# Scaling of the coarse attention probabilities moved from VectorE to GpSimd, with three schedule constants

## The chip, the cores and the metric

One core of a Trainium2 chip runs the whole program: two attentions, their sum and two feed-forward layers. The metric is the device time of one execution in microseconds (us).

## The reference, cut to what matters

Shapes: q, k and v are 2 x 8 x 576 x 64 (batch, heads, positions, head size); the feed-forward layers have 1152 tokens, width 512 and inner width 2048.

```python
q_d = q.reshape(B, H, Sd, factor, D).mean(axis=3)      # factor 4, so Sd = 144; k_d and v_d alike
out_d = sm_attn(q_d, k_d, v_d)                         # softmax attention over 144 coarse positions
out_up = np.repeat(out_d, factor, axis=2)
mask = np.abs(pos[:, None] - pos[None, :]) < factor    # fine attention in a band of 7 positions
...
attn = np.exp(scores)
attn = attn / (np.sum(attn, axis=-1, keepdims=True) + 1e-09)
out_local = np.matmul(attn, v)
x = out_up + out_local                                 # then token by token, heads side by side
h = x @ w_in;  g = P(h) / (Q(h) + 1e-06);  x = g @ w_out      # first layer, rational function
h = x @ w_in2; g = h * np.tanh(softplus(h)); out = g @ w_out2 # second layer
```

The division in the coarse softmax is what the change moves: the kernel multiplies the exponentials by the reciprocal of their sum.

## The kernel before, in words

The kernel is built as a list of tasks with estimated durations, priorities and dependencies (`Plan.add`). A list scheduler (`Plan.run`, L105) then walks through an estimated time and gives each free engine the ready task with the lowest priority number; in that order the instructions are written out. So every engine has a fixed instruction order, chosen once, and on the chip each engine runs its list strictly in order, waiting on semaphores.

Attention is cut into 24 units (`unit`, L550): two heads by 2, 3 or 4 windows of 64 positions. Units 1 to 4 have 4 windows and belong to the first quarter of the tokens, units 5 to 12 to the second (3 and 2 windows in turn), 13 to 16 to the third, 17 to 24 to the fourth. Per unit: TensorE transposes q (L467); VectorE sums q over groups (L595) and GpSimd scales the sums (L610); TensorE forms fine and coarse scores (L630 to L641); VectorE takes maxima (L651, L652); ScalarE takes exponentials with their sums (L658, L662); VectorE takes reciprocals of the five sums (L670, L673). Then two scalings follow: `ns` (L678) of the fine probabilities, 128 x 80 per window, on GpSimd or VectorE as the scheduler finds it; and `npd` (L684) of the coarse ones, 128 x 144, on VectorE. Both precede TensorE's transposes of the probabilities (L696 of the coarse, L700 of the fine), which are copied out of PSUM (L712, L717), multiplied with v (L731 coarse, L737 fine) and added up (L749, L756) into x, which is split in two float32 parts xh (L767/L769) and xl (L772).

`prep` (L469) serves each pair of heads in each batch: k is loaded (L475/L479) and transposed, v is loaded (L530, "vr") and its four-fold sums are formed in two additions (L536, L540) on GpSimd or VectorE. Every load is issued from SyncE's queue (SP): q by L564, the v windows of a unit by L576, the weights by L866 and L871. q has three buffers (`NQN = 3`), so from the fourth q load on a load waits until an earlier unit's q has been transposed.

The feed-forward layers run in steps of two blocks of 128 inner columns: L1003 is the first matmul of a step (three products for float32 accuracy), L1151 and L1153 the second. Weights arrive in a wide format and are decoded by ScalarE and VectorE: L883, L890, L897 (and L903), then split into a high part (L909 on ScalarE or L911 on VectorE) and a low part (L914). The first L1003 of a step needs that step's decoded weights, its x, and a free PSUM buffer. Where TensorE has no task the scheduler may place a filler matmul (L448, 128 x 480 bfloat16, result unused).

What sets the order around the change: the priority of units (`PROL`, `PSTEP` for the first four, `LEAD` for all others, L833 and L835: how far ahead of its feed-forward step a unit is wanted), of the v windows (`VOFF`, L581), of weight decoding (`CLEAD`, L918), and the estimated durations (`t_pool`, `t_dve`, `t_act`).

Of the kernel before, what the change touches and what calls it, by code (L numbers as in the profile page):

```python
# [25 lines left out]
SECOND = 0.8  # L26
COLD, FILL_ALL = 3.4, 20
WINDOW, FILL, FILL_END = 3.4, 0.5, 450.0
LEAD, CLEAD, LLEAD, OLAG = 25, 5, 35, 16
PROL, PSTEP, VOFF, VROFF, LOFF, KOFF = -45, 1.5, 0, 0, 11, 12  # L30
GROUPS = ([6, 6, 4], [4, 4, 4, 4])
KCUT = 4
MKP = -45
# [10 lines left out]
def t_dve(n, fast=False, ptr=0):  # L44
    return 0.068 + n * (0.000521 if fast else 0.001042) + 0.06 * ptr


def t_pool(n, two=True):
    return 0.147 + n * 0.0021 if two else 0.06 + n * 0.00104
# [22 lines left out]
class Plan:  # L72
# [6 lines left out]
    def add(self, engs, fn, prio, after=(), take=(), use=(), chain=None, dens=0.5, port=False):  # L79
        t = Task()  # L80
        t.port = port
        t.dens = dens
        t.engs, t.fn, t.prio, t.take = engs, fn, prio, list(take)
        t.out, t.next, t.started, t.ended, t.seq = [], None, False, False, len(self.tasks)
        t.use = list(take) + list(use)
        deps = set(after)
        for b in take:
            b.owner = t
        for b in use:
            deps.add(b.owner)  # L90
        for b in t.use:
            b.users += 1
        deps.discard(None)
        t.deps = len(deps)
        if chain is not None:
            if chain in self.last:
                self.last[chain].next = t
                t.deps += 1
            self.last[chain] = t
        for d in deps:  # L100
            d.out.append(t)
        self.tasks.append(t)
        return t
# [134 lines left out]
def kernel(  # L238
# [13 lines left out]
    nc = tc.nc  # L252
# [6 lines left out]
    SD = S // 4  # L259
# [4 lines left out]
    add = plan.add  # L264
# [285 lines left out]
    def unit(u, slots, start):  # L550
        bb, p, w0, nw, n, prio = u.bb, u.p, u.w0, u.nw, u.n, u.prio
# [5 lines left out]
        tm, s, pd, pT, pdT, od, xt = (  # L557
            Buf(tm_s), Buf(s_s), Buf(pd_s), Buf(pT_s), Buf(pdT_s), Buf(od_s), Buf(xt_s)
        )
# [66 lines left out]
        def pe_b():  # L626
# [19 lines left out]
            use=[qT, qd], chain="pb",  # L646
# [28 lines left out]
        tc_ = add({"dve": 0.35}, rc, prio, after=[te], use=[tm])  # L675
# [5 lines left out]
            )  # L681

        def npd():
            nc.vector.tensor_scalar(  # L684
                out=pd.v, in0=pd.v, scalar1=tm.v[:, 14:15], scalar2=0.25, op0=ALU.mult,
                op1=ALU.mult,
            )

        tn = [
            add({"pool": t_pool(WK * nw), "dve": t_dve(WK * nw)}, ns, prio, after=[tc_], use=[tm, s], port=True),  # L690
            add({"dve": 0.2}, npd, prio, after=[tc_], use=[tm, pd], port=True),
        ]

        def pe_d():
# [31 lines left out]
        def pe_e():  # L726
# [17 lines left out]
            use=[vw, pT, pdT], chain="pe",  # L744
# [85 lines left out]
    for c in range(4):  # L830
        for i, (bb, p, w0, nw) in enumerate(need[c]):
            if c == 0:
                prio = PROL + PSTEP * i  # L833
            else:
                prio = cstart[c - 1] + (i / len(need[c])) * (cstart[c] - cstart[c - 1]) - LEAD  # L835
            slots = {"half": half_s, "s": sc_s, "pt": pt_s, "po": po_s}
            if c == 0:
                slots = {kk: slots[kk] + early[kk] for kk in slots}
            if (bb, p) not in seen:
                seen.add((bb, p))  # L840
                prep(bb, p, prio - 1, slots, c == 0)
            att_last = unit(Unit(bb, p, w0, nw, prio), slots, c == 0)
# [435 lines left out]
```

## Time and profile before

| | us |
|---|---|
| time, median of 3 runs (lowest to highest) | 513.7 (509.99 to 514.14) |
| the profiled execution | 511.9 |
| its span, first to last instruction | 510.1 |
| TensorE busy | 494.1 (97%) |
| VectorE, ScalarE busy | 351.7 (69%), 346.0 (68%) |
| GpSimd busy | 77.6 (15%) |

The span is the profiled execution without some 1.8 us around it. "Busy" of TensorE is modelled, since matmuls are pipelined. The shares are averages over an attention-heavy first quarter and a second half that is nearly matmuls alone, so they are read by stage below.

### The profile page before, as it was taken

The page shows a single profiled execution, that of the slowest core. Times are in us where ns is not written, and L with a number is a line of the kernel's source. Part 1 is how long each engine was busy: PE and PEld are TensorE (multiplying, and loading weights), DVE is VectorE, ACT ScalarE, POOL GpSimd, SP SyncE. Part 2 cuts the span into 40 slices and gives each one's busy share as a digit, 9 for nine tenths or more (in the row PEclk, how much of TensorE's full clock was granted, in tenths as well). Part 3 has the DMA queues.
Part 4 walks back from the last instruction along what each step waited for, and adds up shares of the span by engine and source line. Part 5 has one row for each costly group of instructions (what it writes and reads, how often), then busy time and mean ns, then how long its engine had stood idle before and what let it go on. Part 6 is the DMA issues. An engine that isn't in the chain of part 4 may idle for free.

```text
span 510.1 us, 8850 instructions
## 1 busy us (share of the span) xinstructions
PE 494.1 (97%) x3503; PEld 447.8 (88%) x3503; DVE 351.7 (69%) x530; ACT 346.0 (68%) x648; POOL 77.6 (15%) x104
## 2 busy tenths in 40 slices
PE   8989999999999999999989999999999999999996
PEld 5668668889999999999979989888998899989995
DVE  4778999899899996898889998925832622221322
ACT  5789997998889999999998999655621422112210
POOL 3644556334000000000000403400000000000000
PEclk9989999999999999999989999999999999999999
DMA  9986835241322242222412224252300000000111
GB/s 179 200 235 179 199 100 183 56 112 45 143 84 84 82 164 84 84 82 84 126 41 84 82 92 156 84 164 84 131 36 0 1 0 1 0 1 0 63 62 62
DMA packets 44313, 46.51 MB, mean 91 GB/s; under 512 B 27760, under 2 KB 30832, under 8 KB 44272
## 3 DMA queue, kind: packets, MB, share of 16 engines
q1 hardware_dynamic: 44272, 45.95, 30.4%
q8 instruction: 27, 0.44, 0.3%
q14 instruction: 14, 0.11, 0.1%
HBM read 43.58 MB, written 2.36 MB: 90 GB/s over the span
## 4 chain that ended last, share of the span: by engine, by line
PE 55%; ACT 23%; DVE 15%; issue 3%; DMA 3%; POOL 0%; SPq 0%; DVEq 0%; POOLq 0%; ACTq 0%
PE psum L1003 22%; PE psum L1153 19%; PE psum L1151 6%; ACT L945 2%; ACT raw L890 2%; ACT wt L883 2%; ACT wrk L1029 2%; DMA att<-in_v_dram 2%; DVE wt L897 1%; ACT att L658 1%; DVE wi L914 1%; DVE wrk L1039 1%; PE psum L467 1%; DMA raw<-in_moe_w_in_dram 1%; PE psum L448 1%
## 5 line engine op out<-in xcount | busy, mean ns | idle before, releaser
L1003 PE MATMUL psum<-xh,wi 128*128 128x384 f32 (+1 forms) x528 | 132.9, 324 | 0.0
L1003 PEld LDWEIGHTS psum<-xh,wi 128*128 128x128 f32 x528 | 93.7, 188 | 1.8 <-issue 1.2
L1003 PE MATMUL psum<-xl,wi 128*128 128x384 f32 (+1 forms) x264 | 84.5, 320 | 0.0
L1003 PE MATMUL psum<-xh,late_r 128*128 128x384 f32 x288 | 77.0, 336 | 2.1 <-DVE late_f L1047 1.2
L1151 PE MATMUL psum<-gg,wo 128*128 128x384 f32 (+1 forms) x456 | 73.7, 316 | 2.7 <-ACT gg L1118 1.7
L1151 PEld LDWEIGHTS psum<-gg,wo 128*128 128x128 f32 x456 | 69.8, 192 | 4.4 <-DVE gg L1123 2.1
L1003 PEld LDWEIGHTS psum<-xh,late_r 128*128 128x128 f32 x288 | 52.4, 188 | 3.5 <-DVE late_f L1047 1.5
L1153 PE MATMUL psum<-wo,gg 128*128 128x512 f32 x216 | 51.0, 391 | 0.0
L1003 PEld LDWEIGHTS psum<-xl,wi 128*128 128x128 f32 x264 | 49.8, 189 | 0.2
L1003 PE MATMUL psum<-xl,late_r 128*128 128x384 f32 x144 | 48.2, 335 | 0.0
L1153 PEld LDWEIGHTS psum<-wo,gg 128*128 128x128 f32 x216 | 40.4, 188 | 8.1
L1097 ACT ACTIVATE late_f<-psum 128x768 f32<-128x768 f32 (+1 forms) x12 | 9.5, 790 | 53.1 <-PE psum L1003 53.1
L897 DVE SCALAR_TENSOR_TENSOR wt<-wt,raw 128x1024 int32<-128x1024 int32 x32 | 40.5, 1269 | 7.0 <-ACT raw L890 3.8
L890 ACT ACTIVATE raw<-raw 128x1024 int32<-128x1024 uint16 x32 | 36.8, 1154 | 9.1 <-DMA raw<-in_moe_w_in_dram 5.8
L1210 POOL TENSOR_TENSOR xl<-part,xh 128x768 fp32r<-128x768 f32 x6 | 15.6, 2616 | 177.2 <-ACT xh L1205 177.2
L883 ACT ACTIVATE wt<-raw 128x1024 f32<-128x1024 f32 x32 | 36.4, 1140 | 7.8 <-DMA raw<-in_moe_w_out_dram 4.0
L1230 DVE TENSOR_TENSOR part<-psum,part 128x512 f32<-128x512 f32 x27 | 18.3, 692 | 32.7 <-PE psum L1153 32.7
L1097 ACT ACTIVATE wrk<-psum 128x768 f32<-128x768 f32 (+1 forms) x13 | 10.3, 790 | 44.6 <-PE psum L1003 44.6
L1123 DVE TENSOR_TENSOR gg<-wrk,gg 128x768 fp32r<-128x768 f32 (+2 forms) x23 | 19.5, 852 | 19.9 <-ACT gg L1097 19.6
L1003 PEld LDWEIGHTS psum<-xl,late_r 128*128 128x128 f32 x144 | 27.0, 188 | 0.3
L1153 PE MATMUL psum<-wo,late_r 128*128 128x512 f32 x108 | 25.6, 390 | 0.0
L1123 DVE TENSOR_TENSOR gg<-late_f,gg 128x768 fp32r<-128x768 f32 x14 | 13.4, 955 | 17.6 <-ACT gg L1097 17.2
(133 smaller groups left out, 980.0 us busy)
## 6 DMA issues: line engine op xcount, KB each, us to landing
raw<-in_moe_w_in_dram SPq DMA_DIRECT2D x16, 1024.0 KB, 5.1
raw<-in_moe_w_out_dram SPq DMA_DIRECT2D x16, 1024.0 KB, 4.9
out_dram<-part SPq DMA_DIRECT2D x9, 256.0 KB, 2.1
att<-in_v_dram SPq DMA_DIRECT2D x32, 60.0 KB, 2.5
att<-in_k_dram SPq DMA_DIRECT2D x6, 288.0 KB, 4.6
att<-in_v_dram SPq DMA_DIRECT2D x6, 256.0 KB, 5.2
att<-in_q_dram SPq DMA_DIRECT2D x16, 96.0 KB, 4.1
att<-in_v_dram SPq DMA_DIRECT2D x8, 80.0 KB, 5.6
```

Source lines behind the costliest of these rows:

```text
L883: nc.scalar.activation(out=t.v, in_=words(r)[:, :, 1].bitcast(F32), func=AF.Prelu if fold else AF.Identity, scale=2.0 ** -112, **({"alpha" ...
L890: nc.scalar.activation(out=words(r)[:, :, 0], in_=r.v.bitcast(U16).rearrange("p (n four) -> p n four", four=4)[:, :, 1], func=AF.Copy, sca ...
L897: nc.vector.scalar_tensor_tensor(out=ti, in0=ti, scalar=3, in1=words(r)[:, :, 0], op0=ALU.logical_shift_left, op1=ALU.bitwise_or)
L945: nc.scalar.preload_act_table_set(name)
L1003: nc.tensor.matmul(st.h.v[:, i, :T], w.v[:, ww, ks], xx[:, kk, c0:c0 + T], start=(nn == 0 and (st.big or i == 0)), stop=(nn == 3 * KD - 1 ...
L1029: nc.scalar.activation(out=vw(st.a), in_=H(), func=AF.Abs)
L1097: nc.scalar.activation(out=vw(dst), in_=H(), func=AF.Mish)
L1123: ENG[e].tensor_tensor(out=vw(st.gl), in0=vw(st.c), in1=vw(st.gh).bitcast(F32), op=ALU.subtract)
L1151: nc.tensor.matmul(A(d)[:, :T], w.v[:, ww, lo + d * 128:lo + (d + 1) * 128], vw(gg)[:, i, :], start=start, stop=stop)
L1153: nc.tensor.matmul(A(d), vw(gg)[:, i, sl], w.v[:, ww, lo:lo + DM], start=start, stop=stop)
L1210: ENG[e].tensor_tensor(out=xl[xs], in0=pv, in1=xh[xs].bitcast(F32), op=ALU.subtract)
L1230: nc.vector.tensor_tensor(out=pv, in0=acc.v[:, j], in1=pv, op=ALU.add)
```

## The change

`npd` is issued on GpSimd, always, with an estimated duration of 0.06 + 144 x 0.00104 = 0.21 us in the scheduler; and three constants of the priorities differ. Since the scheduler makes the whole order anew, all engines' lists move.

```diff
-LEAD, CLEAD, LLEAD, OLAG = 25, 5, 35, 16
-PROL, PSTEP, VOFF, VROFF, LOFF, KOFF = -45, 1.5, 0, 0, 11, 12
+LEAD, CLEAD, LLEAD, OLAG = 35, 5, 35, 16
+PROL, PSTEP, VOFF, VROFF, LOFF, KOFF = -40, 1.5, 4, 0, 11, 12
...
         def npd():
-            nc.vector.tensor_scalar(
+            nc.gpsimd.tensor_scalar(
                 out=pd.v, in0=pd.v, scalar1=tm.v[:, 14:15], scalar2=0.25, op0=ALU.mult,
...
-            add({"dve": 0.2}, npd, prio, after=[tc_], use=[tm, pd], port=True),
+            add({"pool": t_pool(SD, two=False)}, npd, prio, after=[tc_], use=[tm, pd], port=True),
```

Counted over the whole program, TensorE has 63 fillers before and 50 now (39 and 36 of them ahead of the first L1003); VectorE loses 24 L684 and one each of L536 and L712, and gains one each of L540, L607, L678, L769, L1188, L1207, L1210 and two L911; ScalarE loses one each of L605, L767, L1186, L1205 and two L909, and gains one L710; GpSimd gains the 24 L684 and one L536, and loses one each of L540, L678, L1210.

On TensorE, the place where the third feed-forward step begins (its weights are wi_77), before: the attention of the second quarter has its transposes and a filler in front, and the L731 that follow belong to unit 14.

```order
L467 MATMUL psum<-ident,att 128x96 x3
L448 LDWEIGHTS ident_62
L448 MATMUL psum<-mask,ident_62 128x480
L1003 MATMUL psum<-xh,wi_77 128x256
L1003 MATMUL psum<-xl,wi_77 128x256
L1003 MATMUL psum<-xh,wi_77 128x256
L731 MATMUL psum<-att 64x48 x4
```

The same place now: the second step (wi_76) has just ended, and the L696 and L700 in front belong to unit 10.

```order
L1003 MATMUL psum<-xl,wi_76 128x256
L1003 MATMUL psum<-xh,wi_76 128x256
L696 MATMUL psum<-ident,att 72x128 x2
L700 MATMUL psum<-ident,att 80x128 x2
L1003 MATMUL psum<-xh,wi_77 128x256
L1003 MATMUL psum<-xl,wi_77 128x256
L1003 MATMUL psum<-xh,wi_77 128x256
```

The third step moved four units forward; 23 fillers stand between the second step and the third before, and none now; after the first L1003 there are 24 in all before and 14 now (8 ahead of the second step, 5 within the fourth, 1 far later).

On GpSimd, units 1 and 2 before (the first L678 is unit 1's, L536 and L540 are the sums of v):

```order
L536 TENSOR_TENSOR att<-att 72x4x128
L540 TENSOR_TENSOR att<-att 72x2x2x64
L678 TENSOR_TENSOR att<-att 128x320
L610 TENSOR_SCALAR att<-att 128x64
L540 TENSOR_TENSOR att<-wrk 72x2x2x64
L678 TENSOR_TENSOR att<-att 128x320
```

The same place now:

```order
L536 TENSOR_TENSOR att<-att 72x4x128
L678 TENSOR_TENSOR att<-att 128x320
L684 TENSOR_SCALAR att<-att 128x144
L536 TENSOR_TENSOR wrk<-wrk 72x4x128
L684 TENSOR_SCALAR att<-att 128x144
L540 TENSOR_TENSOR att<-wrk 72x2x2x64
```

L684 stands behind L678 of its unit, and both stand, as L678 did before, behind an L536 that waits for a load of v.

On SyncE, the loads that follow the first four of k and three of q, before (L530 is the load for the sums of v, L576 the v windows of a unit):

```order
L564 DMA att<-in_q_dram 128x4x64
L530 DMA att<-in_v_dram 64x4x256
L530 DMA att<-in_v_dram 8x4x256
L576 DMA att<-in_v_dram 80x4x64 x2
L530 DMA wrk<-in_v_dram 64x4x256
L530 DMA wrk<-in_v_dram 8x4x256
L576 DMA att<-in_v_dram 80x4x64 x2
```

The same place now:

```order
L564 DMA att<-in_q_dram 128x4x64
L564 DMA att<-in_q_dram 96x4x64
L530 DMA att<-in_v_dram 64x4x256
L530 DMA att<-in_v_dram 8x4x256
L564 DMA att<-in_q_dram 64x4x64
L530 DMA wrk<-in_v_dram 64x4x256
L530 DMA wrk<-in_v_dram 8x4x256
L564 DMA att<-in_q_dram 96x4x64
```

The q loads of units 5, 6 and 7 moved in front of loads of v, and the v windows of units 1 and 2 moved behind all of these.

## Rows read from the trace of the kernel before

**Rows 1.** Windows by stage: length, busy us of each engine (instructions), PEclk, DMA
```profile
core 0: us, PE busy (x) PEld busy (x) DVE busy (x) ACT busy (x) POOL busy (x), PEclk, DMA share, GB/s
0.00:37.20 37.20, 33.97 (x351) 22.62 (x351) 23.64 (x67) 27.08 (x96) 18.19 (x38) 0.95 0.92 204
37.20:53.80 16.60, 16.58 (x218) 13.98 (x216) 14.04 (x43) 15.35 (x54) 9.24 (x15) 1.00 0.71 175
53.80:74.30 20.50, 18.45 (x236) 12.48 (x235) 19.08 (x51) 19.54 (x72) 10.78 (x16) 1.00 0.59 151
74.30:130.70 56.40, 55.37 (x694) 49.84 (x692) 51.36 (x116) 48.07 (x148) 23.23 (x30) 1.00 0.39 116
130.70:200.00 69.30, 67.87 (x432) 66.91 (x431) 64.99 (x76) 64.92 (x83) 0.61 (x1) 1.00 0.24 85
200.00:262.00 62.00, 59.69 (x339) 58.24 (x338) 50.03 (x52) 59.55 (x67) 0.00 (x0) 1.00 0.31 103
262.00:312.00 50.00, 47.94 (x265) 47.30 (x266) 47.63 (x45) 47.16 (x52) 9.36 (x4) 0.97 0.25 85
312.00:505.00 193.00, 193.00 (x979) 175.75 (x978) 78.99 (x83) 64.37 (x82) 6.20 (x3) 1.00 0.14 47
```
**Rows 2.** Windows of the fillers, L448 alone: PE and PEld busy (count)
```profile
53.80:74.30 20.50, 6.28 (x23) 2.18 (x23) 1.00 0.59 151
74.30:130.70 56.40, 0.72 (x2) 0.10 (x2) 1.00 0.39 116
```
**Rows 3.** Timeline of TensorE: start, us, line, tile, shapes, count
```profile
8.03 1.11 PE L467 MATMUL psum<-ident,att 128*128 128x128 f32 x5
...
13.39 3.61 PE L448 MATMUL psum<-mask,ident 128*128 128x480 bf16 x17
16.84 0.38 PE L696 MATMUL psum<-ident,att 128*72 128x128 f32 x2
...
52.08 0.28 PE L1003 MATMUL psum<-xh,wi 128*128 128x256 f32 x1
...
74.32 0.46 PE L1003 MATMUL psum<-xh,wi 128*128 128x256 f32 x1
```
**Rows 4.** Timeline of VectorE at the end of the gap
```profile
72.88 1.61 DVE L914 TENSOR_TENSOR wi<-wt,wi 128x1024 fp32r<-128x1024 f32 x1
```
**Rows 5.** The scaling's own line, L684: durations, and who waited for it
```profile
L684 DVE TENSOR_SCALAR att<-att x24: 280/521/1292, 15.7 to 126.7; 128x144 f32<-128x144 f32 x24
...
  PEld psum L731: 0.6, 3
  PEld psum L696: 0.3, 1
```
**Rows 6.** Timeline of VectorE: one L684, and one instruction with two SBUF inputs
```profile
15.66 0.74 DVE L684 TENSOR_SCALAR att<-att 128x144 f32<-128x144 f32 x1
...
39.63 1.22 DVE L897 SCALAR_TENSOR_TENSOR wt<-wt,raw 128x1024 int32<-128x1024 int32 x1
```
**Rows 7.** Timeline of GpSimd: start, us, instruction, and idle time before it
```profile
6.71 0.24 POOL L610 TENSOR_SCALAR att<-att 128x64 f32<-128x64 f32 x1 [2.29 <-DVE att L595]
...
13.14 1.26 POOL L536 TENSOR_TENSOR att<-att 72x512 f32<-72x512 f32 x1 [0.64 <-DMA att<-in_v_dram]
...
15.59 0.72 POOL L678 TENSOR_TENSOR att<-att 128x320 f32<-128x320 f32 x1 [0.40 <-ACT att L658]
...
39.88 1.06 POOL L610 TENSOR_SCALAR att<-att 128x48 f32<-128x48 f32 x1 [1.96 <-DVE att L595]
...
43.40 0.22 POOL L610 TENSOR_SCALAR att<-att 128x32 f32<-128x32 f32 x1
```
**Rows 8.** Groups by line of GpSimd, shapes apart
```profile
L678 POOL TENSOR_TENSOR att<-att 128x240 f32<-128x240 f32 x15 | 10.4, 695 | 15.5 <-DVE att L673 10.4 <-ACT att L605 4.2 <-ACT gg L1118 1.0
L610 POOL TENSOR_SCALAR att<-att 128x48 f32<-128x48 f32 x16 | 6.7, 418 | 10.5 <-DVE att L595 9.0 <-DVE att L670 1.3
```
**Rows 9.** Chain that ended last: start, us, piece
```profile
24.59 8.14 DMA att<-in_v_dram
...
76.56 1.22 DVE att L684
```
**Rows 10.** Timeline of SyncE: when loads are issued
```profile
6.84 1.23 SPq L530 DMA_DIRECT2D att<-in_v_dram  x2
```
**Rows 11.** Groups by line, shapes apart, of two operations that change engine
```profile
L909 ACT ACTIVATE wi<-wt 128x1024 fp32r<-128x1024 f32 x7 | 7.5, 1072 | 0.8 <-DVE wt L903 0.8
L1205 ACT ACTIVATE xh<-part 128x768 fp32r<-128x768 f32 x6 | 4.9, 841 | 0.2 <-DVE part L1196 0.2
L911 DVE CAST wi<-wt 128x1024 fp32r<-128x1024 f32 x3 | 2.1, 694 | 3.4 <-PE psum L1003 3.3
```

## Prediction

> **What bounds the kernel now.** I read the stages first, then the matmul engine's gaps, then who was late there. The table of stages [rows 1] shows TensorE busy for all 193 us of the last stage, so nothing that GpSimd or VectorE does can shorten that one. From 74.3 to 312 us it is busy 97 to 98% of each stage except for small idle parts; from 130.7 us on these are 1.43, 2.31 and 2.06 us, 5.8 us together. The loose place is 53.8 to 74.3 us: TensorE idles 20.50 - 18.45 = 2.05 us there, and 23 of its instructions are fillers [rows 2]. A filler costs (16.84 - 13.39) / 17 = 0.20 us from start to start [rows 3], so 4.7 us of that stage are filler and 6.7 us in all are not work. No feed-forward matmul runs from 52.08 to 74.32 us [rows 3]: the third step's weights are completed by an L914 that starts at 72.88 us [rows 4], and the matmul starts before its record ends at 74.49 only because such records overlap by a little. In this gap ScalarE is busy 19.54 of 20.50 us and VectorE 19.08 [rows 1]: both are full, ScalarE a little more. The start, up to the first feed-forward matmul at 37.2 us, is a chain of loads and of the first units, not a question of VectorE, which is busy only 23.64 us of it.
>
> So a microsecond of VectorE is worth something between 37 and 130 us, where it delays TensorE's next input, and little elsewhere.
>
> **The change part by part.**
>
> *VectorE without L684.* 24 instructions with a median of 521 ns, from 280 to 1292 ns [rows 5]. The spread is a wait inside the record. One L684 starts at 15.66 us and takes 0.74 us, just until the L678 that GpSimd began at 15.59 us is through [rows 6, 7]. At the median, 24 x 0.521 = 12.5 us leave VectorE, of which 24 x (0.521 - 0.280) = 5.8 us were such waiting. Most of it is not on the path: TensorE waited for L684 only 0.6 + 0.3 = 0.9 us [rows 5], and the chain that ended last has one piece of it among its long ones, 1.22 us at 76.56 us [rows 9]. I take 1.2 us as the direct gain; the bounds are 0 (another wait ends next, ScalarE being full) and the 5.8 us of waiting.
>
> *The gap.* With the time freed and the new priorities, the scheduler puts the third step's matmuls four units earlier on TensorE, and 14 fillers stand after the first L1003 where 24 stood. 10 fillers fewer are 10 x 0.20 = 2.0 us. The idle time I shorten in the same proportion, 2.05 x 10 / 23 = 0.9 us. Together 2.9 us. Bounds: 0, if ScalarE, which keeps nearly all its work there, makes TensorE stand where fillers stood; 6.7 us, if the whole gap closes.
>
> *GpSimd with L684.* One input, 128 x 144, with a scalar per partition. No row shows that on GpSimd. The nearest is L610, one input with fixed scalars: 0.22 us for 32 columns and 0.24 us for 64 [rows 7], hence 0.24 + 80 x (0.02 / 32) = 0.29 us as an estimate. Bounds: 0.24 us, and the 0.695 us of a two-input L678 with 240 columns [rows 8]. I take 0.29 us because L610 is the same kind of operation. 24 x 0.29 = 7.0 us on an engine that is busy 18.19 of the first 37.2 us and 23.23 of 56.4 us later [rows 1] make it no bound by its load. What it costs is order: L684 now stands behind its unit's L678, so the coarse transposes L696 come 0.29 us after L678 ends instead of about with it. TensorE has other units and feed-forward matmuls to put there, so I book nothing for it; without that cover it is 0.29 us a unit.
>
> A second cost is the other direction of the same waiting. The L610 at 39.88 us takes 1.06 us, to the end of the L897 that VectorE runs from 39.63 to 40.85 us [rows 6, 7]. L610 with 48 columns has a mean of 418 ns [rows 8] beside the 220 to 240 ns of an undisturbed one [rows 7], so I expect L684 to lose some 0.2 us each as well, to a mean of 0.5 us. The page "SBUF — State Buffer" of the Trainium skill, section "SBUF: two separate sides", says more strongly that GpSimd and VectorE take the shared port pair as an exclusive lock, and that whichever comes second is blocked for the whole instruction of the other. This speaks against the change: the waiting would not vanish with L684 but change sides, and by the rule VectorE's two-input instructions would in turn wait behind 24 instructions more. The two pairs of rows above agree with it. What that would cost at its worst is the third rival.
>
> *The start.* The first load for the sums of v is issued at 6.84 us [rows 10], and its L536 starts on GpSimd at 13.14 us, released by that load [rows 7]. In the new order a q load stands in front that needs a q buffer, that is, unit 2's transposes, which end at 8.03 + 1.11 = 9.14 us [rows 3]; with the q load's own issue, some 0.6 us as half of the pair's 1.23 us [rows 10], v goes out at about 9.75 us, 2.9 us later. L536 would start at 16.05 and end 1.26 us later, L678 (0.72 us) and L684 (0.29 us) follow [rows 7]: the first probabilities are ready at 18.3 us, against 16.84 us for the first L696 before [rows 3]. That is 1.5 us late; three fillers fewer before the first L1003 give 0.6 us back. I book +0.9 us. Bounds: 0, since a lighter DMA load early may bring v in sooner; and 2.5 us, if v windows, now behind weight loads, come late as well. A v load issued behind weights took 8.14 us on the chain at 24.59 us [rows 9].
>
> *Elsewhere.* Two L909 of 1.07 us and one L1205 of 0.84 us leave ScalarE, 3.0 us; two L911 of 0.69 us and smaller pieces go to VectorE [rows 11]. From 130.7 to 312 us both are busy nearly all the time, and TensorE idles the 5.8 us named above. I take 1.0 us, a third of what ScalarE loses, because VectorE takes part of it on; bounds 0 and 3.0 us.
>
> **Sum**, against the profiled execution's own 511.9 us (span 510.1 us and 1.8 us around it): -2.9 - 1.2 - 1.0 + 0.9 = -4.2 us, hence 507.7 us. The profiled execution is 0.35% below the median of 513.7 us; against that median the forecast is 1.2% lower.
>
> **The rivals.**
>
> *The gap moves but doesn't close.* ScalarE is 95% busy in the gap, and the change leaves its attention work as it was. Bringing the third step forward brings its activations forward too; TensorE then waits where the fillers were. For it: ScalarE's 19.54 of 20.50 us. Against it: the third step waited for VectorE's L914, not for ScalarE. Then the 2.9 us fall away and half of the 1.2: 511.9 - 0.6 - 1.0 + 0.9 = 511.2 us, no difference that can be measured.
>
> *The gap closes.* The whole 6.7 us, 1.2 us directly, 1.0 us elsewhere, and a start that costs nothing: 511.9 - 8.9 = 503.0 us. For it: in the new order no filler stands between the second and third step. Against it: five fillers and eight still stand nearby.
>
> *GpSimd becomes the chain.* Place: every unit's L678 and L684, in series, in front of TensorE's L696. Price: 0.29 us and 0.2 us of waiting for VectorE, 0.5 us per unit. It decides once TensorE has less other work between a unit's scores and its transposes than this chain lasts. If that holds for the 19 to 20 units after the first L1003: 20 x 0.5 = 10.0 us, with the gap unimproved; 511.9 + 10.0 - 1.0 + 0.9 = 521.8 us, slower. For it: GpSimd runs strictly in its order, and L678 already waits on v loads at the start. Against it: TensorE waited for GpSimd hardly at all before, and feed-forward matmuls are mixed in between.
>
> **How the numbers follow.** A measurement of this kernel tells about 1% from no change; against the median that is 508.6 and 518.8 us. The forecast, with chance 0.50 and its own range 504.5 to 510.5 us, lies below 508.6 us two times in three: 0.33 faster, 0.17 same. The gap moves: 0.22, nearly all same (0.02 faster). The gap closes: 0.13, faster. GpSimd becomes the chain: 0.15, with 0.13 slower and 0.02 where only part of the units pay. Together faster 0.48, same 0.39, slower 0.13. The range from 502.5 to 514.5 us takes in the closed gap and a start at its worst bound beside a gap that only moves (511.2 + 1.6 = 512.8 us), and leaves out most of the last rival.
>
> **What would show it.** Right: the stretch without feed-forward matmuls between 52 and 74 us is gone or less than half, the stage's fillers fall by ten; L684 on GpSimd has a minimum near 0.29 us and a mean near 0.5; the first L696 is about 1.5 us later and the first L1003 up to 1 us later; the last stage is still 193 us long and starts about 4 us earlier. Wrong: TensorE's waits name L684 or L678 for more than 3 us in all (the third rival), or its idle time between 37 and 130 us grows by what the fillers lost (the first). If the first L1003 starts after 39 us, the start was priced too low.

## The result, and the profile after

| | before | after |
|---|---|---|
| time, median of 7 runs each (lowest to highest), us | 513.11 (509.99 to 514.14) | 507.60 (506.18 to 508.95) |
| ratio, 95% interval | | 0.9918 [0.9890, 0.9947] |
| the profiled execution, its span, us | 511.9, 510.1 | 508.95, 506.8 |
| busy: TensorE, VectorE, ScalarE, GpSimd, us | 494.1, 351.7, 346.0, 77.6 | 491.4, 348.7, 344.3, 83.8 |

The change is faster by 0.8%. The forecast was 507.7 us. Measured again later, beside the experiments, it gave 507.62 us and 0.9911 [0.9876, 0.9945]. The time is as forecast; most of the steps are not, and the experiments were made to find out which.

The stages of the changed kernel, cut where [rows 1] cuts the kernel before (same columns):

```profile
0.00:37.20 37.20, 34.89 (x394) 24.04 (x396) 24.13 (x72) 29.20 (x104) 21.96 (x46) 1.00 0.88 210
37.20:53.80 16.60, 15.50 (x189) 11.25 (x186) 13.00 (x34) 14.16 (x47) 8.36 (x14) 0.90 0.77 171
53.80:74.30 20.50, 19.36 (x228) 16.03 (x227) 19.93 (x42) 20.25 (x64) 13.54 (x18) 1.00 0.75 195
74.30:130.70 56.40, 55.22 (x705) 49.71 (x704) 49.69 (x114) 50.38 (x159) 27.93 (x44) 1.00 0.38 109
130.70:200.00 69.30, 67.59 (x417) 65.82 (x417) 63.91 (x73) 64.42 (x80) 0.46 (x1) 1.00 0.27 88
200.00:262.00 62.00, 61.08 (x348) 59.93 (x347) 55.51 (x59) 58.98 (x67) 0.00 (x0) 1.00 0.32 107
262.00:312.00 50.00, 46.80 (x264) 45.19 (x263) 46.96 (x44) 45.65 (x50) 9.34 (x4) 1.00 0.25 85
312.00:505.00 193.00, 190.93 (x964) 173.16 (x962) 75.52 (x81) 61.25 (x77) 2.25 (x1) 1.00 0.13 45
```

From 130.7 to 312 us TensorE idles 181.3 - 175.5 = 5.8 us, as much as before: no waiting was saved there. Its granted clock is 0.90 in the second stage, where it was 1.00 before, 1.00 in the first, where it was 0.95, and 1.00 from 262 to 312 us, where it was 0.97.

TensorE's timeline at the places of [rows 3] (the first L696, the first L1003, the end of the first step, three waits, fillers, the second step):

```profile
15.58 0.38 PE L696 MATMUL psum<-ident,att 128*72 128x128 f32 x2
...
33.27 0.39 PE L1003 MATMUL psum<-xh,wi 128*128 128x256 f32 x1
...
40.59 0.28 PE L1003 MATMUL psum<-xh,wi 128*128 128x256 f32 x1
41.07 0.44 PE L467 MATMUL psum<-ident,att 96*128 96x96 f32 x3 [0.20 <-ACT att L658]
41.77 0.44 PE L731 MATMUL psum<-att 72*64 72x48 f32 x8 [0.26 <-DVE att L756]
42.76 0.94 PE L737 MATMUL psum<-att 80*64 80x64 f32 x12 [0.56 <-DMA att<-in_v_dram]
...
45.23 1.80 PE L448 MATMUL psum<-mask,ident 128*128 128x480 bf16 x4
...
53.21 0.36 PE L1003 MATMUL psum<-xh,wi 128*128 128x256 f32 x1
```

The 22.2 us without an L1003 between 52.08 and 74.32 us are gone, but a stretch of 53.21 - 40.59 = 12.6 us without one now stands before the second step. The fillers alone, as in [rows 2]:

```profile
53.80:74.30 20.50, 1.34 (x5) 0.47 (x5) 1.00 0.75 195
74.30:130.70 56.40, 0.00 (x0) 0.00 (x0) 1.00 0.38 109
```

23 fillers became 5 in that stage; eight more stand between 45 and 51 us. The moved scaling by its own line, for [rows 5]:

```profile
L684 POOL TENSOR_SCALAR att<-att x24: 378/387/1961, 14.9 to 124.2; 128x144 f32<-128x144 f32 x24
...
  PEld psum L696: 1.3, 3
  PE psum L696: 0.7, 2
```

The minimum is 0.378 us (expected 0.29) and the group's mean 14.0 / 24 = 0.58 us (expected 0.5). TensorE waited 0.7 us for it and its weight loads 1.3 us, 2.0 us together; in a second profile of the change (`e5_after_again`) the two are 1.3 and 2.2 us, 3.5 us together. That is over the 3 us that the forecast named as a sign of GpSimd as the chain, yet the kernel is not slower; `e4_after_order_dve` below shows why. The start on GpSimd and on SyncE's queue, for [rows 7, 10]:

```profile
12.50 1.27 POOL L536 TENSOR_TENSOR att<-att 72x512 f32<-72x512 f32 x1 [1.25 <-DMA att<-in_v_dram]
14.16 0.72 POOL L678 TENSOR_TENSOR att<-att 128x320 f32<-128x320 f32 x1 [0.40 <-DVE att L673]
14.87 0.55 POOL L684 TENSOR_SCALAR att<-att 128x144 f32<-128x144 f32 x1
```

```profile
8.55 1.24 SPq L530 DMA_DIRECT2D att<-in_v_dram  x2
```

v was issued 1.7 us later than before, and yet its L536 began 0.64 us earlier: from issue to L536 it took 12.50 - 8.55 = 3.95 us, where before it took 13.14 - 6.84 = 6.30 us. The busy share of the DMA engines from 10 to 14 us is 0.70 to 0.71, where it was 1.19 to 1.24 as the same view counts it: the lighter load early on that the forecast had as its bound of 0.

So in this pair of profiles the first L1003 comes 37.20 - 33.27 = 3.9 us earlier, the span is 3.3 us shorter, and all of that lies ahead of the first L1003, where the forecast had a loss of 0.9 us. TensorE has the same matmuls to do ahead of it in both orders, line for line, apart from three fillers. What differs there is idle time and the clock. Windows of TensorE in the kernel before (length, busy us, count, granted clock, DMA share, GB/s):

```profile
32.00:33.00 1.00, 0.23 (x2) 1.00 0.49 129
...
33.50:36.50 3.00, 3.00 (x23) 0.50 0.87 261
```

and in the changed kernel:

```profile
41.00:43.00 2.00, 1.11 (x13) 1.00 0.82 180
...
44.50:48.00 3.50, 3.50 (x16) 0.53 0.57 125
```

These are spells at 1.2 GHz (0.50), some 3 to 3.5 us long, and each follows a stretch in which TensorE was partly idle. The changed kernel's comes after the wait for v windows at 42.76 us, whose loads `VOFF` ranks lower (that this made them late is not shown); so it lies behind the first L1003 while that of before lies ahead of it. It recurs in a second profile of the changed kernel (`e5_after_again`, 44 to 48 us). The kernel before has a second spell, from 262 us on, where the changed kernel has none:

```profile
262.00:265.00 3.00, 2.80 (x9) 0.50 0.00 0
```

One pair of profiles can't say what the change is worth; that needs the runs below.

### The profile page after: what moved, and what is told of

Same layout as the page of the kernel before. It is cut to its first block, busy times and chain, and to the rows that moved or that the text cites. A ratio compares the mean times of both kernels' runs of the same rounds, so it can differ in the third digit from the quotient of the medians.

```text
span 506.8 us, 8818 instructions
## 1 busy us (share of the span) xinstructions
PE 491.4 (97%) x3490; PEld 445.1 (88%) x3490; DVE 348.7 (69%) x513; ACT 344.3 (68%) x643; POOL 83.8 (17%) x126
## 4 chain that ended last, share of the span: by engine, by line
PE 58%; ACT 24%; DVE 13%; DMA 2%; POOL 1%; issue 1%; DVEq 0%; POOLq 0%; ACTq 0%
PE psum L1003 23%; PE psum L1153 19%; PE psum L1151 6%; ACT L945 4%; ACT wrk L1029 2%; ACT raw L890 2%; ACT wt L883 2%; ACT late_f L1032 2%; ACT late_f L1024 2%; PE psum L467 1%; PE psum L636 1%; PE psum L737 1%; ACT late_f L961 1%; PE psum L731 1%; ACT late_f L956 1%
## 5 line engine op out<-in xcount | busy, mean ns | idle before, releaser
L1003 PE MATMUL psum<-xh,wi 128*128 128x384 f32 (+1 forms) x528 | 132.7, 324 | 0.0
L1003 PEld LDWEIGHTS psum<-xh,wi 128*128 128x128 f32 x528 | 93.6, 188 | 1.5 <-issue 1.0
L1003 PE MATMUL psum<-xl,wi 128*128 128x384 f32 (+1 forms) x264 | 84.5, 320 | 0.0
L1003 PE MATMUL psum<-xh,late_r 128*128 128x384 f32 x288 | 77.0, 336 | 1.8 <-DVE late_f L1047 1.8
L1151 PE MATMUL psum<-gg,wo 128*128 128x384 f32 (+1 forms) x456 | 73.5, 313 | 0.4 <-DVE gg L1123 0.3
L1151 PEld LDWEIGHTS psum<-gg,wo 128*128 128x128 f32 x456 | 68.6, 189 | 2.5 <-DVE gg L1123 1.4
L1003 PEld LDWEIGHTS psum<-xh,late_r 128*128 128x128 f32 x288 | 52.4, 188 | 2.9 <-DVE late_f L1047 1.6
L1003 PEld LDWEIGHTS psum<-xl,wi 128*128 128x128 f32 x264 | 49.8, 189 | 0.2
L1003 PE MATMUL psum<-xl,late_r 128*128 128x384 f32 x144 | 48.3, 335 | 0.8 <-POOL xl L1210 0.8
L897 DVE SCALAR_TENSOR_TENSOR wt<-wt,raw 128x1024 int32<-128x1024 int32 x32 | 41.6, 1300 | 7.2 <-ACT raw L890 6.4
L1210 POOL TENSOR_TENSOR xl<-part,xh 128x768 fp32r<-128x768 f32 x5 | 11.6, 2324 | 175.0 <-ACT xh L1205 174.5
L1123 DVE TENSOR_TENSOR gg<-wrk,gg 128x768 fp32r<-128x768 f32 (+1 forms) x22 | 18.8, 854 | 24.2 <-ACT gg L1097 22.9
L1003 PEld LDWEIGHTS psum<-xl,late_r 128*128 128x128 f32 x144 | 27.0, 188 | 1.4 <-POOL xl L1210 1.1
L1123 DVE TENSOR_TENSOR gg<-late_f,gg 128x768 fp32r<-128x768 f32 (+1 forms) x15 | 15.3, 1022 | 14.4 <-ACT gg L1097 13.8
```

Source lines behind the costliest of these rows:

```text
L897: nc.vector.scalar_tensor_tensor(out=ti, in0=ti, scalar=3, in1=words(r)[:, :, 0], op0=ALU.logical_shift_left, op1=ALU.bitwise_or)
L1003: nc.tensor.matmul(st.h.v[:, i, :T], w.v[:, ww, ks], xx[:, kk, c0:c0 + T], start=(nn == 0 and (st.big or i == 0)), stop=(nn == 3 * KD - 1 ...
L1123: ENG[e].tensor_tensor(out=vw(st.gl), in0=vw(st.c), in1=vw(st.gh).bitcast(F32), op=ALU.subtract)
L1151: nc.tensor.matmul(A(d)[:, :T], w.v[:, ww, lo + d * 128:lo + (d + 1) * 128], vw(gg)[:, i, :], start=start, stop=stop)
L1210: ENG[e].tensor_tensor(out=xl[xs], in0=pv, in1=xh[xs].bitcast(F32), op=ALU.subtract)
```

## The experiments

The question: is it the engine (L684 off VectorE), the constants, or the order that the scheduler happens to make of both? Each engine's list can be kept while one instruction is issued elsewhere, since the list is fixed before it runs. All times are medians of the runs given, in us; each of the three sets of four shared one chip and its own runs of the kernel before: 510.44 (30 runs), 511.70 (30) and 512.26 (33). A ratio comes from the comparison with those runs and is not quite the quotient of the two medians: it lies up to 0.003 away from it.

**First set: engine, constants, order.** `e1_move_only` keeps the old constants and moves L684; `e2_consts_only` keeps L684 on VectorE with the new constants; both are planned anew.

```diff
 # e1_move_only, against the change
-LEAD = 35; PROL = -40; VOFF = 4
+LEAD = 25; PROL = -45; VOFF = 0
 # e2_consts_only, against the kernel before
-LEAD = 25; PROL = -45; VOFF = 0
+LEAD = 35; PROL = -40; VOFF = 4
```

> L684 on GpSimd, the three constants as before, the order made anew. Before is 513.1 us, the change 507.6. Two theories. Order: what was gained is the early start (first L1003 at 33.3 us where it was at 37.2), which comes from loads in another order, and this kernel keeps the old order of loads: 511 to 514 us, first L1003 between 36 and 38 us. Engine: what was gained is VectorE's time without L684: 507 to 509 us, wherever the first L1003 lies.

Measured: 512.77, ratio 1.0051 [1.0029, 1.0073], 12 runs.

> The three constants of the change, L684 on VectorE as before, the order made anew. Order theory: q loads go out before the v loads as in the change, so the first L1003 comes by 34.5 us and the whole takes 508 to 510 us. Engine theory: 512 to 515 us, since VectorE has all its work again and 68 fillers stand in the list where the change has 50.

Measured: 514.18, ratio 1.0091 [1.0058, 1.0124], 7 runs. Neither half of the change gains anything alone; both lose. The gain is not a sum of the two. The time of `e1_move_only` lies where the order theory had it and that of `e2_consts_only` where the engine theory had it, so neither theory holds for both. The first L1003 starts at 34.40 us in `e1_move_only` and at 30.70 us in `e2_consts_only`, earlier than the 33.27 us of the change: an early start alone is not the gain.

The other two kernels of the set keep an order and change only the engine on which L684 is issued.

```diff
 # e3_before_order_pool: the kernel before, every list as it was
-            nc.vector.tensor_scalar(
+            nc.gpsimd.tensor_scalar(
 # e4_after_order_dve: the change, every list as it was
-            nc.gpsimd.tensor_scalar(
+            nc.vector.tensor_scalar(
```

> The order of before on every engine, instruction by instruction, but each L684 is written to GpSimd's list at the point where it stood in VectorE's. So the engine alone changes. Order theory: 512 to 514.5 us, within 0.3% of before. Engine theory: 508 to 510.5 us. If GpSimd's chain costs something, 515 us or more.

Measured: 512.29, ratio 1.0034 [1.0004, 1.0065], 12 runs.

> The order of the change on every engine, but each L684 is written to VectorE's list at the point where the scheduler put it on GpSimd's. Order theory: 506.5 to 508.5 us, as the change. Engine theory: 511 to 514 us.

Measured: 507.88, ratio 0.9956 [0.9926, 0.9985], 12 runs. In the order of before the engine alone gains nothing and costs 0.3%. The order with L684 back on VectorE keeps a gain of 0.4%. How that compares with the change is not settled, since the two never ran in one set: its time is the change's own (507.60 and 507.62 in other sets), but this set's runs of the kernel before have the lowest median of all, so its ratio is half as far from 1, with an interval that meets those of the change. L684's line in `e3_before_order_pool`, and the first line of engine times of its profile:

```profile
L684 POOL TENSOR_SCALAR att<-att x24: 378/385/817, 15.5 to 125.0; 128x144 f32<-128x144 f32 x24
...
  PEld psum L696: 2.6, 5
...
PE 490.4 (97%) x3503; PEld 444.2 (88%) x3503; DVE 343.2 (68%) x506; ACT 345.9 (68%) x648; POOL 89.2 (18%) x128
```

and the same two views of `e4_after_order_dve`:

```profile
L684 DVE TENSOR_SCALAR att<-att x24: 279/286/1327, 15.5 to 124.3; 128x144 f32<-128x144 f32 x24
...
  PEld psum L696: 2.0, 4
  PE psum L696: 0.9, 3
...
PE 488.5 (96%) x3490; PEld 442.5 (87%) x3490; DVE 354.1 (70%) x537; ACT 344.1 (68%) x643; POOL 71.2 (14%) x102
```

In the order of before VectorE is busy 351.7 - 343.2 = 8.5 us less without L684, not the 12.5 us of the forecast, so its other instructions grew longer; TensorE's weight loads wait 2.6 us for L684 where they waited 0.9 us in [rows 5]. In the new order TensorE and its weight loads wait 2.9 us for L684 on VectorE, between the 2.0 and 3.5 us for L684 on GpSimd: these waits come with the order, not with the engine.

**Second set: the scaling left out, and the fillers.** `e5_after_again` is the change itself. `e8_before_order_no_scale` keeps the order of before and leaves the scaling of the coarse probabilities out altogether, so its price is measured with no other engine to pay it. `e6_before_nofill` and `e7_after_nofill` keep their orders and leave out the fillers behind the first L1003 (24 and 14; their results are used by nothing).

```diff
 # e8_before_order_no_scale
-            nc.vector.tensor_scalar(out=pd.v, ...)
+            pass
 # e6_before_nofill; e7_after_nofill has 44 for 47
-                    fns[-1](s.view)
+                    self.nfill += 1; fns[-1](s.view) if self.nfill <= 47 else None
```

> The change itself once more, beside the others. If the gain is the order, it lies 0.990 to 0.995 of before, as the first measurement (0.9918). If part of the first gain was only that before's clock was lowered more often in those runs, it comes nearer to 0.996, and runs at a mean granted clock of 0.999 or more differ by about 2 us: 509.1 us for before in the last session, 507.3 for the change's order with L684 on VectorE.

Measured: 507.62, ratio 0.9911 [0.9876, 0.9945], 7 runs. The ratio is as the order theory had it. At a mean granted clock of 0.999 or more the change takes 507.23 (4 runs) and before 510.80 (7), 3.6 us apart and not the 2 us expected.

> Before, its order kept, with L684 left out altogether: the coarse probabilities are not divided by their sum. It bounds what taking L684 off VectorE can give in this order. Theory engine: the 12.7 us taken from VectorE count in part, 1.2 us (the prediction's term) to 5.8 us less than before, 0.989 to 0.998. Theory order: the attention units are paced by ScalarE and by the fixed order, so within 0.2% of before.

Measured: 512.19, ratio 0.9993 [0.9964, 1.0022], 12 runs. Even without the 24 instructions the kernel before is no faster by anything that can be measured; VectorE is busy 342.0 us in its profile, 9.7 us less. The interval alone still admits the 1.2 us of the forecast (0.2%); for the move as a whole `e3_before_order_pool` doesn't.

> Before, its order kept, without the 24 fillers that stand behind the first L1003. Theory cost (a term of the prediction): each filler costs its 0.20 us, so 4 to 5 us less than before. Theory idle: they stand in time in which TensorE waits anyway, so 0.998 to 1.002 of before, and the stage from 54 to 75 us has some 4.7 us more idle time. Theory clock: TensorE rests in the gap, the granted clock falls to 1.2 GHz in some places after it, 1 to 4 us more than before and a lower mean clock.

Measured: 515.13, ratio 1.0051 [1.0019, 1.0083], 12 runs.

> The change, its order kept, without the 14 fillers behind the first L1003. Cost: 2 to 3 us less than the change. Idle: within 0.2% of the change. Clock: 1 to 3 us more than the change, with a lower mean clock.

Measured: 512.37, ratio 0.9987 [0.9951, 1.0023], 12 runs, 4.8 us above the change by the medians and 3.9 us by the ratios. Leaving work out makes both kernels slower, as the clock theory had it, the change by more than the 1 to 3 us expected. Windows of TensorE in `e6_before_nofill`:

```profile
56.00:58.00 2.00, 1.05 (x9) 1.00 0.34 69
...
60.00:70.00 10.00, 10.00 (x100) 0.50 0.55 112
70.00:75.00 5.00, 3.99 (x30) 0.50 0.42 103
```

and in `e7_after_nofill` (all engines; the first pair behind the length is TensorE's, the clock is the figure before the DMA share):

```profile
48.00:50.00 2.00, 1.14 (x16) 0.99 (x18) 1.91 (x6) 2.00 (x11) 0.68 (x2) 0.95 0.60 146
50.00:60.00 10.00, 10.00 (x86) 8.43 (x84) 7.49 (x17) 7.46 (x27) 5.45 (x9) 0.50 0.85 225
```

Where the fillers stood, TensorE now waits for the same inputs, and then runs real matmuls at 1.2 GHz for 10 us and more: 100 of them in the 10 us from 60 us on in the one kernel, 86 in the 10 us from 50 us on in the other, and 129 in the next 10 us, when the clock is back. Each of the two had one run at a mean granted clock of 0.999 or more: 510.15 and 506.58, close to the 510.80 and 507.23 of the kernels with their fillers. So by these two runs TensorE waits about as long without the fillers as they took, and what is lost on top is the clock. A filler is not 0.20 us to be saved. The page "TensorE: Matmul & The Clock Gate" of the Trainium skill, section "What's actually happening", says that the throttled state is the default one and activity lifts it; these rows agree.

**Third set: one constant back at a time, and more fillers.**

```diff
 # e9_prol45          # e10_voff0        # e11_lead25
-PROL = -40           -VOFF = 4          -LEAD = 35
+PROL = -45           +VOFF = 0          +LEAD = 25
 # e12_after_fill2: each of the 14 late fillers issued twice
-                    fns[-1](s.view)
+                    self.nfill += 1; (fns[-1](s.view), fns[-1](s.view) if self.nfill > 44 else None)
```

> The change with one constant set back: PROL -45 for -40 (the first four units are wanted earlier again); L684 stays on GpSimd and the order is made anew. TensorE's list has 65 fillers for 50. Theory (the gain belongs to one order, not to one constant): a ratio to the kernel before of 0.996 to 1.006, so most of the 0.9% is gone. Rival A (the gain comes from LEAD, which pulls units and so the third step forward): 0.989 to 0.994 stays, since LEAD is kept. Rival B (the gain is the later start of the first units, PROL): 1.000 or above here, while the two kernels beside it keep 0.99.

Measured: 517.90, ratio 1.0084 [1.0050, 1.0119], 12 runs.

> The change with VOFF set back to 0 for 4 (the v windows of a unit no longer yield to other loads). 53 fillers for 50. Theory: 0.994 to 1.004; a constant that touches only the order of some loads leaves more of the change's order standing than the others, so if any of the three keeps the gain it is this one. Rival (the gain comes from q loads ahead of v windows): 1.000 or above here and here alone.

Measured: 517.61, ratio 1.0082 [1.0055, 1.0108], 12 runs.

> The change with LEAD set back to 25 for 35. 58 fillers for 50. Theory (no constant alone): 0.996 to 1.006. Rival A (LEAD alone carries the gain): 1.000 or above here, 0.989 to 0.994 in the two kernels that keep LEAD 35. If the ratio here stays at 0.991, the third step's place, which LEAD sets, is not where the gain comes from.

Measured: 518.17, ratio 1.0102 [1.0068, 1.0136], 12 runs. Each rival had needed two of the three to keep 0.99, and none does; the theory (no constant alone) holds, but its ranges were too low: setting any one constant back costs 1.6 to 1.9 points of ratio, and leaves a kernel slower than before. Of the combinations that were run, this one alone carries the gain. Where about half of the loss lies was not expected either. The row for the stage from 130.7 to 200 us, first in `e9_prol45`:

```profile
130.70:200.00 69.30, 63.28 (x425) 61.16 (x424) 64.94 (x78) 61.85 (x88) 2.58 (x4) 0.99 0.27 92
```

in `e10_voff0`:

```profile
130.70:200.00 69.30, 61.52 (x402) 59.37 (x401) 60.23 (x72) 58.91 (x83) 2.51 (x4) 0.97 0.27 92
```

and in `e11_lead25`:

```profile
130.70:200.00 69.30, 62.95 (x431) 60.64 (x428) 62.82 (x77) 60.28 (x85) 3.68 (x5) 0.99 0.28 94
```

Against 67.87 and 67.59 us of before and after, 4 to 6 us more of idle time, in a stage that holds the end of the attention (the last L684 starts at 134 us in these three, at 124.2 us in the change) and else feed-forward steps alone. By the ratios they lose 8 to 10 us to the change; where the rest of it lies was not located. In `e9_prol45` TensorE's timeline shows one long wait there:

```profile
193.71 0.34 PE L1003 MATMUL psum<-xh,late_r 128*128 128x384 f32 x1
197.53 0.45 PE L1003 MATMUL psum<-xh,late_r 128*128 128x384 f32 x1 [3.49 <-ACT late_f L1032]
```

with a spell at a lower clock in the 4.5 us behind it (windows of TensorE as above):

```profile
194.00:197.50 3.50, 0.05 (x1) 1.00 0.70 289
197.50:200.00 2.50, 2.46 (x10) 0.68 0.00 0
200.00:202.00 2.00, 2.00 (x8) 0.55 0.00 0
```

and ScalarE's timeline shows what stands ahead of L1032, which reads the PSUM of an earlier step:

```profile
187.97 1.28 ACT L945 ACT_TABLE_LOAD   x1
...
191.93 1.28 ACT L945 ACT_TABLE_LOAD   x1
...
196.58 0.90 ACT L1032 ACTIVATE late_f<-psum,b_sb 128x768 f32<-128x768 f32 x1 [1.08 <-DVE late_f L1047]
```

Two table loads (for the logarithm and the sigmoid) with two activations behind each, and two other activations, stand in front of it in ScalarE's list; its last 1.08 us it waits for VectorE's L1047. When the first load begins, TensorE has 6 us of L1003 left that are free to run. In the changed kernel the same group begins at 178.76 us, while TensorE has the rest of an L1151 and then L1003 until 187.7 us (187.41 + 0.34), 9 us, beside it; TensorE idles 1.03 us in all behind it, waiting for L1118 and L1123. The other two kernels wait 3.4 us at the same L1032. So constants of the priorities of attention units and their loads also change how a table load at 180 to 190 us falls against TensorE's work.

> The change's order with each of the 14 fillers behind the first feed-forward matmul issued twice (28 for 14). Theory (fillers stand in time in which TensorE would wait, and keep its clock up): +0.0 to +1.0 us on the change's 507.6 us, ratio 0.991 to 0.994, and the spell at 1.2 GHz near 45 us shorter or gone. Rival (each filler costs its 0.20 us, as the prediction's gap term had it): 14 x 0.20 = +2.8 us, 510.4 us, ratio 0.996 to 0.997, in the runs at full clock too.

Measured: 509.41, ratio 0.9915 [0.9883, 0.9948], 10 runs; by the bare medians it is 509.41 / 512.26 = 0.994, where the change has 507.62 / 511.70 = 0.992, some 1.2 us apart. The interval of the comparison leaves the 0.996 of the rival out. The runs at a mean granted clock of 0.999 or 1.000 say the same: 507.95 here (6 runs) beside 511.62 for before (8), a ratio of 0.993; in the second set the change had 507.23 (4 runs) beside 510.80 (7), also 0.993. Fourteen more fillers cost nothing that shows in runs at full clock and some 1.2 us by the medians, less than half of the rival's 2.8 us. Its windows where the change ran at 1.2 GHz:

```profile
42.00:44.00 2.00, 2.00 (x36) 1.00 0.71 149
44.00:46.00 2.00, 2.00 (x14) 1.00 0.95 184
46.00:48.00 2.00, 2.00 (x35) 1.00 1.02 385
```

The spell is gone from this execution, whose span is 505.0 us beside the change's 506.8. But the time isn't better than the change's by any measure of all runs, so no kernel of the study beats it.

## Why the prediction was right, and where it wasn't

The sum came out (-4.2 us forecast; -5.5 us in the first runs, -4.1 us in the second set), by terms of which most did not: that it came so near is in good part luck. Two of its readings of [rows 1] are off: from 74.3 to 312 us TensorE is busy 96 to 98% of each stage, not 97 to 98, and VectorE is busy 81% from 200 to 262 us, not nearly all the time. No term is worked out from either.

*The gap (-2.9 us).* Its sign was right, its working was not. The third step did move and 23 fillers became 5 in that stage. But "10 fillers fewer are 2.0 us" failed: `e6_before_nofill` and `e7_after_nofill` show that a filler taken away leaves a wait about as long and often a lower clock, and `e12_after_fill2` that a filler added costs little or nothing. What the new order gains is read best in runs at full clock (0.999 or more). With L684 on VectorE in both, in one set: before 509.12 (10 runs) and `e4_after_order_dve` 507.32 (10), 1.8 us. With L684 on GpSimd in both, but in different sets: `e3_before_order_pool` 509.76 (4) and the change 507.2 to 507.3 (4 runs in each of two), 2.5 us. Before and the change themselves, in the second set: 510.80 and 507.23, 3.6 us. So it is 1.8 to 3.6 us; whether the engine or the chip is behind the difference of these figures is open. The profiles don't show the gain as less idle time of TensorE: it idles 510.1 - 494.1 = 16.0 us before and 15.4 us after, 17.0 us in `e3_before_order_pool` and 18.1 us in `e4_after_order_dve`. With the fillers (63 and 50, at 0.20 us) it is 28.6 and 25.4 us, 29.6 and 28.1 us, so 1.5 to 3.2 us less. If fillers stand in waits, as the experiments say, TensorE waits less in the new order, and fewer fillers are a sign of that and not its cause.

*L684 off VectorE (-1.2 us).* This step failed in the order of before: the move costs 0.3% there and leaving L684 out gains nothing. The 12.5 us that were to leave VectorE were 8.5 us of busy time, and the 0.9 us that TensorE's weight loads had waited for L684 came back as 2.6 us of waiting for it on GpSimd. The bound of 0, "another wait ends next", was the answer. In the new order it isn't settled: at full clock the times don't differ (507.32 and 507.2 to 507.3), but by the ratios to before (0.9956 beside 0.9911 to 0.9918) some 0.4% could still come with L684 on GpSimd. The two kernels side by side in one set would tell.

*Elsewhere (-1.0 us).* Failed: nil, 5.8 us of idle time before and after. ScalarE's fewer instructions saved no waiting there; that its share of the time doesn't set TensorE's waits one for one is the likely reading, and was not tested. What differs in that stretch is the second spell of the kernel before.

*The start (+0.9 us).* The loss didn't come. The step that failed is "2.9 us later" for v, carried over whole to L536. In the profile the load went out 1.7 us later and landed sooner, 3.95 us after its issue in place of 6.30 us; `e3_before_order_pool` (order of before) and `e4_after_order_dve` (new order) show the same, 7.03 and 4.47 us. The 3.9 us that the pair of profiles shows at the first L1003 are not the worth of the order: in those two experiments, whose profiles show no spell there, the first L696 starts at 15.90 and 15.86 us and the first L1003 at 34.93 and 35.06 us. One list ahead of the first L1003 also scatters between profiles: it starts at 33.38 us in `e6_before_nofill` and 37.20 us before, at 32.96 us in `e12_after_fill2` and 35.77 us in `e7_after_nofill`. A difference of 1 us between the two orders would not be seen.

*What the sum lacked.* The clock. Over all runs, not the profiled ones alone, the changed kernel's median of the mean granted clock is 0.999 to 1.000, and that of before is 0.997. What that is worth shows within one kernel: before, in the third set, took 511.62 us at 1.000 (8 runs) and 516.71 and 514.95 us at 0.987 (2 runs), some 4 us for 0.013. By that, 0.002 to 0.003 is an estimated 0.6 to 1 us. This fits what the runs at full clock leave of the difference of the medians: 2.6 - 1.8 = 0.8 us for `e4_after_order_dve`, 4.1 - 3.6 = 0.5 us for the change.

*L684 on GpSimd.* Estimated 0.29 us at its shortest from L610's fixed scalars; measured 0.378 us, 35% more than VectorE's 0.279 us in `e4_after_order_dve`. "GPSIMD Engine Reference" of the Trainium skill, section "4.1 Engine selection", calls one-input operations roughly line rate; for this instruction that is generous. The forecast that the waiting would change sides held: maximum 1.96 us and mean 0.58 us, against VectorE's 0.52 us median before.

*The rivals.* "The gap moves but doesn't close" had part of the mechanism (VectorE and ScalarE are fuller than before in that stage, 19.93 and 20.25 of 20.50 us) but not the time, nor its sign: TensorE's idle time from 37.2 to 130.7 us is 3.1 us before and 3.4 us after, far from what the fillers lost. "GpSimd becomes the chain" fell with the times, though its sign was met in one of two profiles (3.5 us): the same order with L684 on VectorE has 2.9 us. The sign "less than half of the 52 to 74 us" was not quite met: that stretch went, but one of 12.6 us stands in front of the second step.

Open: why the new order waits less. Each neighbour loses 4 to 6 us in one feed-forward stage; which of its many moved instructions is behind the gain was not isolated, nor where in the kernel the gain lies.

## What to carry to other kernels

Where a scheduler remakes the whole order, a moved instruction is priced with its list held fixed, and the new list is priced with the instruction put back. Here the first gained nothing and the second 0.4%, and no part of the change kept the gain alone. Fillers in TensorE's idle time are not time to be won: price the wait behind them, and the clock that they hold up. Relief of an engine that is 93% busy in a stage, as VectorE is in the gap, can be worth nothing if TensorE was not waiting for it.

## What was not expected of the hardware

Taking unused matmuls out cost 2.6 and 3.9 us by the ratios, with the granted clock at 0.50 for stretches of 10 us and more. The clock can fall without a long idle piece: in the changed kernel the three waits ahead of the spell were 0.20, 0.26 and 0.56 us, with TensorE busy 1.11 of 2 us. Nor do the same waits always bring a spell: the kernel before waits 1.72 and 0.38 us at two L1151 ahead of and in its second one, and `e3_before_order_pool`, with the same list, waits 1.69 and 0.37 us at the same two and keeps its full clock.

The kernel before spends 1.79 us outside its span, and `e3_before_order_pool`, the same lists with L684 on GpSimd, 2.2 us; 0.4 us of the move's cost lie there, where no view of the profile shows them. The change spends 2.1 to 2.2 us. The engine alone doesn't set this: `e9_prol45`, with L684 on GpSimd too, spends 1.75 to 1.85 us.
